# The first two tiles of an attention step change places in program order

## The chip, the core and the metric

The kernel runs on one core of a Trainium2 chip. A core has five engines with an instruction queue each: TensorE (PE, the matrix unit; its weight loads are shown as PEld), VectorE (DVE), ScalarE (ACT), GpSimd (POOL) and SyncE (SP, which issues most DMAs). Engines meet through semaphores. The metric is the time of one execution on the device in microseconds; the median of several runs is compared.

## The reference

A layer norm feeds two branches that are multiplied at the end: attention with 32 heads of 16 dimensions over 2048 tokens, and a gelu feed-forward of width 1376 with a silu on top.

```python
def _A_ref(x, wqkv, wo):           # S = 2048, D = 512, H = 32, Dh = 16
    qkv = (x @ wqkv).reshape(B, S, 3, H, Dh).transpose(2, 0, 3, 1, 4)
    q, k, v = qkv[0], qkv[1], qkv[2]
    scores = jnp.einsum("bhqd,bhkd->bhqk", q, k) * (Dh ** -0.5)
    p = _softmax(scores, axis=-1)
    o = jnp.einsum("bhqk,bhkd->bhqd", p, v)
    return o.transpose(0, 2, 1, 3).reshape(B, S, D) @ wo

xn = _layernorm(x, axis=-1)
s = _A_ref(xn, A_wqkv, A_wo)
g = _silu(_B_ref(xn, B_w1, B_b1, B_w2, B_b2))
return x + s * g
```

## The kernel before

Everything is in fp32 with operands rounded to a fast fp32 form; where accuracy asks for it a number is kept as a high and a low part, laid one below the other in the contraction (three times 16 rows make the 48 rows of a score matmul).

Attention is cut into 32 units. A unit `u` is a group of four heads (`u // 4`) and a chunk of 512 queries (`u % 4`). For each unit two things are computed from queries and keys:

- Row scores, to find the maximum of each query's scores before any exponential is taken. A tile of 128 queries by 512 keys is one matmul (`s_mm`, line 183) into a PSUM bank, and VectorE reduces it to maxima (`s_max`, line 189). When a unit has its 64 tiles, its maxima are reduced once more and negated (`nm`, line 247), split on GpSimd (lines 250 and 251), turned round by a matmul (`s_end1`, line 267), copied (`mh`, line 277) and sent through DRAM into two extra rows of the unit's queries. So the row scores of a unit have to be done before its transposed scores.
- Transposed scores, 128 keys by 512 queries, with the negated maximum added by those two rows (50 rows in all). `t_one` (line 732) does one matmul (line 739) into a PSUM bank and one exponential on ScalarE (line 741) into `slot`. Those exponentials are multiplied by the values in `pv_step` (line 798): 4 matmuls in the code, 8 on the engine (line 804), on column quarters of the array, with all 128 rows. After 16 key tiles the sum is taken out by ScalarE (`os`, line 811).

The first half of the kernel does the projections, the feed-forward and the row scores of the first nine units. The second half is one loop of 512 steps (line 966, 16 steps for each unit), and all of the change lies there. A step does four transposed tiles of a key tile (one for each head), the `pv` product of the step before, and as many row-score maxima as are due: `due(n) - due(n - 1)` is 3 in nearly all steps until the maxima are used up, and 0 in the last ones. `ORDER` spells the program order of such a step by letters:

- `T`, four times: `t_one`. The first two (T0, T1) use rows 64 to 113 of the array, the last two (T2, T3) rows 0 to 49.
- `S`, twice: a whole 512-wide row-score tile with its maximum; the first of a step (S0) is on rows 0 to 47, the second (S') on rows 64 to 111.
- `X` and `Y`: the two 256-wide halves of a third row-score tile, X on rows 0 to 47, Y on rows 64 to 111, into one bank; the maximum follows Y. Y is held until X is done.
- `V`: `pv_step` of the step before, and then, when it is due, the `s_end1` matmul of a unit.

Matmuls on different halves of the rows can run at the same time, and each brings its own weight load. The scheduling is by hand (`manual_schedule`): what the loop calls first stands first in each engine's queue. PSUM banks go round in rings. Row scores have three banks (`s_ring`), so S' of a step takes the bank of the third maximum of the step before, and S0 that of the S0 before. Transposed tiles have four (`t_tile`, line 724: one of `ps_m`, three of `ps_t`), so each takes the bank of the same tile of the step before, whose exponential must have read it.

Other work hangs on the tiles of a step by `todo`: what is put at position `i` is issued right behind tile T`i`. At position 0 there are `o_move` (DMAs on SP) and `o_den` (line 830: a reciprocal on VectorE, line 832, and two DMAs on SP), each once a unit; the loads of keys, queries and maxima are at position 3.

```python
    for n in range(L + 1):
        ua, ka = divmod(n, 16)
        want = due(n) - due(n - 1)
        i = 0
        for op in ORDER[want] if n > 1 else ("TTTTV", "TTSTSVT")[n]:
            if op in "SXY":
                s_op(op)
            ...
            else:
                if EARLY <= 4 * n + i < 4 * L:
                    t_one(ua, ka, i % 2, 1 - i // 2)
                for f, args in todo.get((n, i), []):
                    f(*args)
                i += 1
```

Of the kernel before, what the change touches and what calls it, by code (L numbers as in the profile page):

```python
# [36 lines left out]
FILL0 = 30  # L37
HB = 4
W2B = 2
ORDER = {0: "TTTTV", 3: "STXTTSTYV"}  # L40
HC = CH // 2
PAIRED = 28
KB = 3
# [5 lines left out]
def fused(ctx: ExitStack, tc: tile.TileContext, x, wqk, wv, wo, w1, b1, w2, b2, out):  # L49
# [916 lines left out]
# [6 lines that stand above are left out]
# [67 lines left out]
```

## Time and profile before

| | us |
|---|---|
| median of 3 runs | 1590.65 (1590.64 to 1590.91) |
| the profiled execution | 1590.04 |
| its span, first to last instruction | 1588.3 |

The granted TensorE clock was 1.0 throughout. A row of the page's first part gives an engine's busy time, its share of the span and its number of instructions. A row of the stretches gives, after the length, the busy time and count of each engine (or of one source line alone), then the granted clock, the busy share of the DMA engines and GB/s. A row of the timeline gives start, duration, engine, line, operation, output and inputs with shapes, how many instructions were merged into it, and in brackets idle time of the engine before it with the engine that the profile names as the releaser. Busy times of neighbours overlap, since engines are pipelined: an exponential lasts about 0.6 us and the next can start about 0.5 us after it.

### The profile page before, as it was taken

The numbers are of one execution on the slowest core, as the hardware profiler recorded it, in microseconds if no ns is written. First come the engines' busy times: TensorE is split into PE (matmuls) and PEld (weight loads), VectorE is DVE, ScalarE is ACT, GpSimd is POOL, SyncE is SP. The second block draws the span as 40 slices with busy tenths as digits, with TensorE's granted clock in tenths as the row PEclk, the third lists the DMA queues.
The fourth block names the chain that finished last, engine by engine and source line by source line (L and its number), as shares of the span: only waits on it lengthen the run. The fifth ranks groups of instructions, "written<-read, shape, count | busy, mean of one in ns | idle before, by whom it ended". The sixth has DMA issues, their size and how long they took to land.

```text
span 1588.3 us, 31761 instructions
## 1 busy us (share of the span) xinstructions
PE 1581.8 (100%) x12144; PEld 934.7 (59%) x12144; DVE 1379.1 (87%) x2261; ACT 1259.1 (79%) x2520; POOL 373.7 (24%) x394
## 2 busy tenths in 40 slices
PE   9999999999999999999999999999999999999998
PEld 8899999999894444444444444444444444444445
DVE  7599898989889999999999999999999999999734
ACT  4334343434349999999999999999999999999984
POOL 4145575756640011001000100100100000000143
PEclk9999999999999999999999999999999999999999
DMA  6626343454332123112410511411150111110252
GB/s 206 150 59 161 109 137 99 157 139 134 114 96 59 37 42 59 28 38 47 76 31 25 70 41 30 62 39 29 33 76 21 32 29 36 36 29 22 59 192 101
DMA packets 74648, 116.87 MB, mean 74 GB/s; under 512 B 23012, under 2 KB 24292, under 8 KB 73320
## 3 DMA queue, kind: packets, MB, share of 16 engines
q1 hardware_dynamic: 70748, 101.89, 23.7%
q0 software_dynamic: 3264, 12.35, 4.5%
q8 instruction: 96, 1.57, 0.4%
q10 hardware_dynamic: 484, 0.60, 0.1%
q14 instruction: 56, 0.46, 0.1%
HBM read 84.35 MB, written 25.97 MB: 69 GB/s over the span
## 4 chain that ended last, share of the span: by engine, by line
PE 97%; ACT 1%; DVE 1%; issue 0%; DMA 0%; ACTq 0%; DVEq 0%
PE pv L804 33%; PE ps L183 24%; PE ps L590 12%; PE pst L739 10%; PE pst L590 7%; PE ps L739 3%; PE ps L80 3%; PE pv L590 2%; PE ps L458 1%; ACT slot L741 1%; PE pst L80 1%; DVE st L417 0%; PE pst L440 0%; DMA xt<-in_x 0%; PE pst L458 0%
## 5 line engine op out<-in xcount | busy, mean ns | idle before, releaser
L189 DVE TENSOR_REDUCE mx<-ps 128x2 f32<-128x512 f32 x2048 | 1299.5, 684 | 144.6 <-PE pst L739 35.2
L741 ACT ACTIVATE slot<-pst 128x512 f32<-128x512 f32 x1533 | 831.7, 614 | 17.8 <-PE pst L739 9.6
L804 PE MATMUL pv<-slot,vsb 128*32 128x512 f32 x4096 | 545.4, 605 | 0.0
L183 PEld LDWEIGHTS ps<-kt,slot 48*128 48x128 f32 x1364 | 223.8, 184 | 280.2 <-DVE mx L189 278.3
L183 PE MATMUL ps<-kt,slot 48*128 48x512 f32 x1364 | 379.4, 365 | 0.0
L739 PE MATMUL pst<-qt,kt 50*128 50x512 f32 x1149 | 376.0, 436 | 0.5 <-DVE gt L672 0.3
L741 ACT ACTIVATE slot<-ps 128x512 f32<-128x512 f32 x515 | 316.5, 615 | 2.5 <-PE ps L183 0.2
L590 PE MATMUL ps<-slot,w1h 64*128 64x512 f32 x1088 | 218.1, 393 | 0.0
L739 PEld LDWEIGHTS pst<-qt,kt 50*128 50x128 f32 x1149 | 188.6, 184 | 41.8 <-ACT slot L865 12.6
L183 PE MATMUL ps<-kt,qz 48*128 48x512 f32 x512 | 212.7, 415 | 0.0
L183 PEld LDWEIGHTS ps<-slot,slot 48*128 48x128 f32 x598 | 98.3, 184 | 121.5 <-DVE mx L189 120.7
L183 PE MATMUL ps<-slot,slot 48*128 48x512 f32 x598 | 166.0, 364 | 0.0
L739 PE MATMUL ps<-qt,kt 50*128 50x512 f32 x387 | 162.7, 422 | 0.0
L590 PEld LDWEIGHTS ps<-slot,w1h 64*128 64x128 f32 x1088 | 151.5, 185 | 8.4 <-ACT junk L604 2.6
L804 PEld LDWEIGHTS pv<-slot,vsb 128*32 128x32 f32 x4096 | 80.8, 108 | 109.2 <-issue 100.2
L590 PE MATMUL ps<-slot,w1l 64*128 64x512 f32 x544 | 141.9, 393 | 0.0
L377 POOL TENSOR_TENSOR hl<-hg,hh 128x512 fp32r<-128x512 f32 x76 | 96.8, 1295 | 129.7 <-ACT hh L376 85.9
L250 POOL CAST nmh<-nm 128x16 fp32r<-128x16 f32 x32 | 6.3, 196 | 477.4 <-DVE nm L247 409.3
L739 PE MATMUL pst<-qt,slot 50*128 50x512 f32 x384 | 113.4, 421 | 0.0
L604 ACT ACTIVATE junk<-ident_r 1x1 f32<-1x1 f32 x92 | 18.0, 196 | 116.5 <-PE pst L590 113.3
L183 PEld LDWEIGHTS ps<-kt,qz 48*128 48x128 f32 x512 | 93.8, 183 | 16.3
L842 POOL TENSOR_TENSOR ot<-ot,dn 64x512 f32<-64x512 f32 x15 | 19.6, 1304 | 299.7 <-DMA dn<-den_d 256.9
(159 smaller groups left out, 1757.7 us busy)
## 6 DMA issues: line engine op xcount, KB each, us to landing
raw<-in_w SPq DMA_DIRECT2D x88, 256.0 KB
qk_h<-hh SPq DMA_DIRECT2D x32, 256.0 KB
qk_l<-hl SPq DMA_DIRECT2D x32, 256.0 KB
qt<-qk_h SPq DMA_DIRECT2D x128, 64.0 KB
slot<-qk_h SPq DMA_DIRECT2D x92, 64.0 KB
g_d<-gt POOLq DMA_DIRECT2D x16, 256.0 KB, 3.5
qt<-qk_l SPq DMA_DIRECT2D x64, 64.0 KB
dn<-den_d SPq DMA_DIRECT2D x32, 128.0 KB
```

The costliest lines, as they stand in the source:

```text
L80: nc.tensor.matmul(ps, lhs[a], rhs[b], start=first and n == 0, stop=last and n == 2)
L183: return nc.tensor.matmul(ps[:, c0:c0 + w], QS[u][r, p, qi * P:(qi + 1) * P], kts[u // NCH % KB][p][r, k0:k0 + w], start=True, stop=True).ins
L189: nc.vector.tensor_reduce(MX[u][:, 2 * p:2 * p + 2, qi, ki][:, heads, parts], ps.rearrange("p (n c) -> p n c", c=HC), axis=AX.X, op=OP.max)
L250: nc.gpsimd.tensor_copy(hl[:, 0], nm)
L377: nc.gpsimd.tensor_sub(hl, raw, hh.bitcast(F32))
L458: nc.tensor.matmul(pq["q", g, c], W1[g][i][:, k * P:(k + 1) * P], (xh, xl)[j][c][:, k], start=n == 0 and k == 0, stop=n == 2 and k == KT - 1)
L590: i = nc.tensor.matmul(ps, lhs[r], rhs[r], start=first, stop=last).ins
L604: i = nc.scalar.activation(junk[:, :1], ident_r[:1, :1].bitcast(F32), AF.Copy).ins
L739: nc.tensor.matmul(ps, kts[g % KB][p][r, k * P:(k + 1) * P], QT[u][r, p, :], start=True, stop=True)
L741: nc.scalar.activation(PT[u, k][:, 2 * p + a, :], ps, AF.Exp, scale=SCALE)
L804: nc.tensor.matmul(PV[u][32 * j:32 * j + 32, :], vsb[:, k, h:h + 32], PT[u, k][:, j, :], start=(k == 0), stop=(k == NT - 1))
L842: eng.tensor_mul(ot[c][rs, g // 2], ot[c][rs, g // 2], DN.pop(u)[rs])
```

## The change

In the order of a step with three maxima the first two letters change places: T0 is issued ahead of S0, where it was issued behind it. What hangs on T0 (position 0) is then also ahead of S0. Everything else, the number of instructions, the banks and the waits of each instruction, stays.

```diff
-ORDER = {0: "TTTTV", 3: "STXTTSTYV"}
+ORDER = {0: "TTTTV", 3: "TSXTTSTYV"}
```

## The prediction

> **What bounds the kernel now.** I read the page first, then busy time over the stage that the change touches, then a few steps in the timeline, at last windows so narrow that merged runs fall apart into single instructions.
>
> ```profile
> span 1588.3 us, 31761 instructions
> PE 1581.8 (100%) x12144; PEld 934.7 (59%) x12144; DVE 1379.1 (87%) x2261; ACT 1259.1 (79%) x2520; POOL 373.7 (24%) x394
> ```
>
> The next three rows are one stretch: all engines, then TensorE's line 804 alone, then ScalarE's line 811 alone.
>
> ```profile
> 498.00:1500.00 1002.00, 1002.00 (x7709) 451.92 (x7705) 916.93 (x1507) 992.11 (x1954) 75.07 (x124) 1.00 0.20 40
> ...
> 498.00:1500.00 1002.00, 512.05 (x3848) 75.76 (x3848) 1.00 0.20 40
> ...
> 498.00:1500.00 1002.00, 18.95 (x30) 1.00 0.20 40
> ```
>
> A step issues 8 matmuls at line 804, so the stretch holds 3848 / 8 = 481 steps, nearly all with the changed order: 2.08 us each. PE is busy 100%, ACT 99%, DVE 92%. Three engines near full mean that a share names no owner; the steps must be followed.
>
> ```profile
> 1001.06 1.07 PE L804 MATMUL pv<-slot,vsb 128*32 128x512 f32 x8
> 1002.06 0.18 PEld L183 LDWEIGHTS ps<-slot,slot 48*128 48x128 f32 x1 [0.84 <-DVE mx L189]
> ...
> 1003.08 1.07 PE L804 MATMUL pv<-slot,vsb 128*32 128x512 f32 x8
> ...
> 1004.07 0.18 PEld L183 LDWEIGHTS ps<-slot,slot 48*128 48x128 f32 x1 [0.84 <-DVE mx L189]
> ...
> 1005.16 1.07 PE L804 MATMUL pv<-slot,vsb 128*32 128x512 f32 x8
> 1006.16 0.18 PEld L183 LDWEIGHTS ps<-slot,slot 48*128 48x128 f32 x1 [0.84 <-DVE mx L189]
> ```
>
> Call the steps A (from 1002.06), B (1004.07) and C (1006.16). The label at a step's first load names DVE, but the load comes 1.00, 0.99 and 1.00 us behind the start of the pv group before it, whatever DVE does: it waits for the pv group to leave the array. What varies is the way from that load to the next pv group: 1.01 to 1.02 us in A, 1.09 in B. Fast and slow steps alternate, 2.02 and 2.08 from pv to pv, 4.10 a pair. Why is B slow?
>
> ```profile
> 1002.06 0.49 PE L183 MATMUL ps<-slot,slot 48*128 48x512 f32 x1
> 1002.06 0.50 PE L739 MATMUL pst<-qt,kt 50*128 50x512 f32 x1
> ...
> 1002.59 0.69 DVE L189 TENSOR_REDUCE mx<-ps 128x2 f32<-128x512 f32 x1 [0.20 <-PE pst L739]
> 1002.62 0.60 ACT L741 ACTIVATE slot<-pst 128x512 f32<-128x512 f32 x1
> ...
> 1003.12 0.59 ACT L741 ACTIVATE slot<-pst 128x512 f32<-128x512 f32 x1
> 1003.59 0.60 ACT L741 ACTIVATE slot<-ps 128x512 f32<-128x512 f32 x1
> 1004.07 0.62 ACT L741 ACTIVATE slot<-pst 128x512 f32<-128x512 f32 x1
> ...
> 1004.74 0.18 PEld L739 LDWEIGHTS pst<-qt,kt 50*128 50x128 f32 x1
> 1004.75 0.18 PEld L183 LDWEIGHTS ps<-slot,slot 48*128 48x128 f32 x1
> 1004.76 0.47 PE L739 MATMUL pst<-qt,kt 50*128 50x512 f32 x1
> ```
>
> A's first pair starts together on the two row halves. DVE takes up the S tile at 1002.59, ACT the T tile at 1002.62. ACT then runs A's four exps, 0.50, 0.47 and 0.48 apart; the fourth ends at 1004.07 + 0.62 = 1004.69. B's fourth T needs that bank (four T banks in turn), and its weights load at 1004.74, 0.05 later. Its matmul shows 0.47 instead of the usual 0.40: it really ran 0.07 late. The pv group at 1005.16 waits for it. So a ScalarE chain over two steps sets the pair:
>
> 0.56 (pair to first exp) + 1.45 (to the fourth) + 0.62 (it) + 0.05 + 0.42 (T load to pv) + 1.00 (pv to the next pair) = 4.10 us, from 1002.06 to 1006.16.
>
> TensorE alone needs 2 x 2.01 = 4.02. The ACT chain owns the difference.
>
> **The change, part by part.** Nothing is added or removed; in every step with three maxima T0 goes ahead of S0. They sit on different row halves (T0 on 64 to 113, S0 on 0 to 47), both behind the same pv drain. Behind them X, T1, T2, S', T3, Y keep their order, S0 still uses the same bank and T0 too, so no bank is asked for earlier than now. On PE the swap is free but for the tiny lag between two pair starts (both print 1002.06, so under 0.01): X follows S0 on its half and inherits it in fast steps. Bounds 0 to 240 x 0.01 = 2.4 us; I take 0.7.
>
> What moves is who is served first. In the program matmul completions are counted by one counter, in order: DVE waits for S0's count, ACT for T0's. Today S0 is the first count, and ACT starts 0.03 behind DVE. The next step shows the same:
>
> ```profile
> 1004.61 0.69 DVE L189 TENSOR_REDUCE mx<-ps 128x2 f32<-128x512 f32 x1
> 1004.64 0.60 ACT L741 ACTIVATE slot<-pst 128x512 f32<-128x512 f32 x1
> ```
>
> The matmuls' lengths (0.49, 0.50) explain a hundredth of it; the rest I read as the spacing of two completions. Swapped, ACT starts 0.03 earlier and DVE 0.03 later. The ACT chain becomes 4.07.
>
> The Trainium skill ("TensorE: Matmul & The Clock Gate", section "The cost: per-tile semaphore tail") says that semaphore increments of concurrent matmuls are written one after another, about 26 ns each, and that matmuls finish in program order. These rows agree with a spacing, at 0.03; by 0.026 the pair gain below would be 5.5 us instead of 6.3.
>
> DVE now pays. Its chain from A to C:
>
> ```profile
> 1003.20 0.68 DVE L189 TENSOR_REDUCE mx<-ps 128x2 f32<-128x512 f32 x1
> ...
> 1003.79 0.68 DVE L189 TENSOR_REDUCE mx<-ps 128x2 f32<-128x512 f32 x1
> ...
> 1004.53 0.18 PEld L183 LDWEIGHTS ps<-slot,slot 48*128 48x128 f32 x1
> ...
> 1004.65 0.40 PE L183 MATMUL ps<-slot,slot 48*128 48x512 f32 x1
> ...
> 1004.89 0.28 PE L183 MATMUL ps<-slot,slot 48*128 48x256 f32 x1
> ...
> 1002.87 0.28 PE L183 MATMUL ps<-slot,slot 48*128 48x256 f32 x1
> ```
>
> A's third max ends at 1004.47 and frees the bank of B's S', whose weights load at 1004.53. From there: at most 0.12 to its matmul, 0.24 to Y, 0.21 from Y to pv (1002.87 to 1003.08 in A, where nothing else is late), 1.00: C's pair could stand at 1006.10, a chain of 4.04. Plus 0.03: 4.07, level with ACT's new 4.07. The 0.12 is an upper end (T1 ahead on the same half ends about there too); by T3, whose matmul really began 0.09 behind its load, it is 4.04. So DVE has just enough room, and a regular pair falls from 4.10 to 4.07.
>
> How many pairs? Line 811 runs 30 times in the stretch, once per 16 steps: an extra ACT instruction.
>
> ```profile
> 810.54 0.63 ACT L811 ACTIVATE os<-pv 128x512 f32<-128x512 f32 x1
> ...
> 811.01 0.65 ACT L741 ACTIVATE slot<-ps 128x512 f32<-128x512 f32 x1
> ```
>
> There the exps follow `os` on ACT at 0.47, not T0's completion, so that step gains nothing. Of the 15 others 7 pairs gain: 30 x 7 x 0.03 = 6.3 us (4.2 to 8.4 with 0.02 to 0.04, as rows are rounded).
>
> The work hung on T0 (position 0: `o_move`, `o_den`) also moves ahead of S0. Its DMA issues keep their place: the SP and POOL sequences come out unchanged. The reciprocal of `o_den` moves one max forward on DVE:
>
> ```profile
> 794.22 0.69 DVE L189 TENSOR_REDUCE mx<-ps 128x2 f32<-128x512 f32 x1 [0.23 <-PE ps L739]
> 794.83 0.24 DVE L832 RECIPROCAL dr<-dr 128x16 f32<-128x16 f32 x1
> 794.99 0.63 DVE L189 TENSOR_REDUCE mx<-ps 128x2 f32<-128x512 f32 x1
> ```
>
> Today it pushes the second max from 0.61 to 0.77 behind the first, 0.16 in DVE's chain. Ahead of the first max it falls into the idle 0.23 and is hidden; without that cover it would cost 30 x 0.16 = 4.8 at most if DVE owned those pairs. What it waits for, `dr`, was sent eight steps before. Bounds: a gain of 0 to 3.0 (30 x (0.16 - 0.06, DVE's room under 4.10)); I take 0.6, since only recips in the first step of a pair matter. Against it, each unit has DVE extras (`nm`, `mh`) where DVE may already own a pair and the 0.03 is a loss: 0 to 60 x 0.03 = 1.8; I take 0.9.
>
> Sum: -6.3 + 0.7 - 0.6 + 0.9 = -5.3 us. The profiled execution took 1590.04 (span 1588.3): 1584.7. It lies 0.6 under the median 1590.65, so against the runs I forecast 1585.3.
>
> **The rivals.**
> - No change: the third chain closes the gap. If fast steps lengthen by what slow ones lose (X's lag nearer 0.01, S' at 0.12, DVE extras at their upper ends), -4.2 + 2.4 + 1.8 = 0: 1590.65. For it: three engines over 90%. Against: ACT's chain stands 0.08 a pair above TensorE's own 4.02.
> - DVE becomes the owner: slower. It decides once S' starts more than 0.15 behind its load (4.04 - 0.12 + 0.03 + 0.15 = 4.10). With the full 0.18 of a load before the matmul the DVE chain is 4.13: +0.03 x 210 = +6.3, 1597. For it: that load already follows the max by 0.06. Against: the row has 0.12, and T3's 0.09.
> - X stalls behind S0. S0 and X now stand next to each other in program order on one row half.
>
> ```profile
> 1002.17 0.19 PEld L183 LDWEIGHTS ps<-slot,slot 48*128 48x128 f32 x1
> ```
>
> X's load starts at 1002.17, inside S0's matmul, so today it is hidden. If it came only behind S0's matmul, X, T2 and T3 would be up to 0.18 later in each step: 481 x 0.18 = 87 us, 1677. Against: T0 between them is on the other half and can't be what hides it. The Trainium skill (same page, section "The mechanism") has a load overlap a running matmul only where the row groups differ; that row shows an overlap within one row half, so the measurement decides.
>
> **How the numbers follow.** A measurement of this kernel can tell 0.2%, 3.2 us, from no change. Forecast 0.70, of which 0.02 falls short of 3.2 us; no change 0.19; DVE the owner 0.09; X stalls 0.02. Faster 0.68, same 0.21, slower 0.11. Range: low end all gains at their upper bounds (-8.4 - 0.6 = -9.0): 1581.6; high end the no-change case: 1590.7. That leaves out the two slower rivals and the largest recip gain.
>
> **What would show it.** Right: in a step's first pair ACT starts ahead of DVE by 0.03; two steps from load to load take 4.07; the fourth T's load still comes 0.05 behind the exp's end; reciprocals lie before a step's first max; idle time of DVE before its maxima changes, PE stays 100%. Wrong: ACT still behind DVE (the spacing belongs to the tile, not the order); pairs still 4.10 with S' late; any fast step above 2.05; loads of X behind 0.3 us.

## The result and the profile after

| | median, us | runs |
|---|---|---|
| before | 1590.64 | 1590.40 to 1590.91 |
| after | 1583.54 | 1583.10 to 1584.09 |

The ratio is 0.9956 with a 95% interval of 0.9943 to 0.9968: 7.1 us or 0.44% faster. The profiled execution after the change took 1583.63 us. The first rows of its page:

```profile
span 1581.8 us, 31761 instructions
...
PE 1574.7 (100%) x12144; PEld 944.7 (60%) x12144; DVE 1382.3 (87%) x2261; ACT 1257.0 (79%) x2520; POOL 373.3 (24%) x394
```

The shares say nothing: TensorE is still "100%" busy. Where the time went is seen in the view of one source line, here line 804 (count, shortest, middle and longest duration in ns, then the start of its first and last instruction in us). Before:

```profile
L804 PE MATMUL pv<-slot,vsb x4096: 592/593/618, 477.5 to 1566.7; 128*32 128x512 f32 x196
```

After:

```profile
L804 PE MATMUL pv<-slot,vsb x4096: 592/593/618, 477.8 to 1560.1; 128*32 128x512 f32 x196
```

The loop took 1089.2 us from its first pv to its last, and takes 1082.3: 6.9 of the 7.1 us lie in it. Now the timeline of the kernel after, cut so narrow that single instructions show; a slow step starts at 1000.91, the next at 1002.98, the one behind it at 1004.99.

```profile
1000.68 0.68 DVE L189 TENSOR_REDUCE mx<-ps 128x2 f32<-128x512 f32 x1
1000.89 0.62 ACT L741 ACTIVATE slot<-pst 128x512 f32<-128x512 f32 x1
1000.91 0.18 PEld L739 LDWEIGHTS pst<-qt,kt 50*128 50x128 f32 x1 [0.84 <-ACT slot L741]
1000.91 0.50 PE L739 MATMUL pst<-qt,kt 50*128 50x512 f32 x1
1000.92 0.49 PE L183 MATMUL ps<-slot,slot 48*128 48x512 f32 x1
...
1001.42 0.18 PEld L183 LDWEIGHTS ps<-slot,slot 48*128 48x128 f32 x1
1001.45 0.60 ACT L741 ACTIVATE slot<-pst 128x512 f32<-128x512 f32 x1
1001.48 0.43 PE L183 MATMUL ps<-slot,slot 48*128 48x512 f32 x1
1001.49 0.69 DVE L189 TENSOR_REDUCE mx<-ps 128x2 f32<-128x512 f32 x1
1001.56 0.18 PEld L739 LDWEIGHTS pst<-qt,kt 50*128 50x128 f32 x1
...
1001.60 0.46 PE L739 MATMUL pst<-qt,kt 50*128 50x512 f32 x1
...
1002.98 0.18 PEld L739 LDWEIGHTS pst<-qt,kt 50*128 50x128 f32 x1 [0.84 <-ACT slot L741]
...
1004.99 0.18 PEld L739 LDWEIGHTS pst<-qt,kt 50*128 50x128 f32 x1 [0.84 <-ACT slot L741]
```

Three things are to be seen. ScalarE now takes up the first tile at 1001.45, 0.03 to 0.04 ahead of VectorE at 1001.49, where it was 0.03 behind. The fourth T still waits for ScalarE: the fourth exponential of the step before ends at 1000.89 + 0.62 = 1001.51, the weights load at 1001.56, the matmul shows 0.46 instead of 0.39 to 0.40. The pair from 1000.91 to 1004.99 takes 4.08, where the one shown before took 4.10. VectorE is close behind: the third maximum ends at 1001.36, S' loads at 1001.42, and its matmul too is a little stretched (0.43).

The rows shown are typical. Over some 400 steps of the loop in the two traces, the median lead is 0.034 for VectorE before and 0.035 for ScalarE after; the fourth T's load comes 0.05 behind the end of the exponential of its bank in both; and the median pair of the stretch 498 to 1500 takes 4.11 before and 4.08 after. The traces also hold the times at which the matmuls' counter was raised: before, for S0 at 1002.567 and for T0 at 1002.601; after, for T0 at 1001.426 and for S0 at 1001.461. Nowhere in either trace do two of these counts lie closer than 0.034.

A label shows how little a releaser's name can mean: the first load of a step used to sit idle 0.84 us "for DVE", now it sits idle 0.84 us "for ACT". The load comes 0.99 to 1.00 us behind the start of the pv group either way (here 1001.99 to 1002.98), so it is the same wait. The name is that of the semaphore that the first tile's load carries: VectorE's for S0, ScalarE's for T0.

### The profile page after: what moved, and what is told of

The parts are those of the page before. It is cut to its first block, busy times and chain, and to the rows that moved or that the text cites. A ratio compares the mean times of both kernels' runs of the same rounds, so it can differ in the third digit from the quotient of the medians.

```text
span 1581.8 us, 31761 instructions
## 1 busy us (share of the span) xinstructions
PE 1574.7 (100%) x12144; PEld 944.7 (60%) x12144; DVE 1382.3 (87%) x2261; ACT 1257.0 (79%) x2520; POOL 373.3 (24%) x394
## 4 chain that ended last, share of the span: by engine, by line
PE 98%; DVE 1%; DMA 0%; issue 0%; ACT 0%; DVEq 0%
PE pv L804 33%; PE pst L739 22%; PE ps L590 13%; PE ps L183 9%; PE pst L590 7%; PE ps L739 7%; PE ps L80 3%; PE pv L590 2%; PE ps L458 1%; PE pst L80 1%; DVE st L417 0%; PE pst L440 0%; DMA xt<-in_x 0%; PE pst L458 0%; DVE slot L75 0%
## 5 line engine op out<-in xcount | busy, mean ns | idle before, releaser
L739 PEld LDWEIGHTS ps<-qt,kt 50*128 50x128 f32 x387 | 71.1, 184 | 45.6 <-ACT slot L741 39.8
```

The lines of the kernel that those rows point to most:

```text
L739: nc.tensor.matmul(ps, kts[g % KB][p][r, k * P:(k + 1) * P], QT[u][r, p, :], start=True, stop=True)
```

## The experiments

Each time stands beside runs of the kernel before on the same chip, whose median lay between 1590.23 and 1590.54.

**1 and 2: the two tiles, and what hangs on T0, each alone.** In the first only the tiles change places, in the second only the hung work (`o_move`, `o_den`) moves ahead of S0.

```diff
 # tiles only (order TSXTTSTYV)
             if op in "SXY":
                 s_op(op)
+                if op == "S" and i == 1:
+                    for f, args in todo.pop((n, 0), []):
+                        f(*args)
...
-                for f, args in todo.get((n, i), []):
-                    f(*args)
+                if i or want != 3:
+                    for f, args in todo.get((n, i), []):
+                        f(*args)
```

```diff
 # hung work only (order STXTTSTYV)
             if op in "SXY":
+                if op == "S" and i == 0:
+                    for f, args in todo.pop((n, 0), []):
+                        f(*args)
                 s_op(op)
```

> T0 ahead of S0, but what hangs on T0 (o_move, o_den with its reciprocal) stays behind S0 as in the kernel before. Theory (the order of the first two completions moves ScalarE's chain forward by 0.03): nearly the whole gain stays, 1583.5 to 1585, since the reciprocal was costed at 0.6 us. Rival (the gain comes from the hung work, above all 30 reciprocals that move into DVE's idle time): back at 1589 or above.

> S0 ahead of T0 as before, but what hangs on T0 goes ahead of S0. Theory: 1590 to 1590.7, only the reciprocals' 0 to 0.6 us are gained. Rival (the hung work makes the gain): near 1584.

Measured: the tiles alone 1585.22 us (1584.97 to 1585.27; ratio 0.9967, 0.9955 to 0.998), the hung work alone 1589.99 (ratio 0.9997, 0.9988 to 1.0006). So the tiles bring 5.2 us and the hung work by itself nothing that is clear of noise, 0.5. But together they bring 7.1, not 5.7: behind the swapped tiles the hung work is worth 1.7 to 1.9 (1.7 between the two medians, whose run ranges don't meet; 1.9 when each is taken against its own runs of the kernel before). The reason is the reciprocal. With the tiles alone it still stands between a step's first and second maximum; VectorE's rows, then the first loads of the steps:

```profile
991.76 0.69 DVE L189 TENSOR_REDUCE mx<-ps 128x2 f32<-128x512 f32 x1 [0.17 <-PE ps L183]
992.37 0.24 DVE L832 RECIPROCAL dr<-dr 128x16 f32<-128x16 f32 x1
992.53 3.14 DVE L189 TENSOR_REDUCE mx<-ps 128x2 f32<-128x512 f32 x5
...
991.19 0.18 PEld L739 LDWEIGHTS pst<-qt,kt 50*128 50x128 f32 x1 [0.84 <-ACT slot L741]
993.21 0.18 PEld L739 LDWEIGHTS pst<-qt,kt 50*128 50x128 f32 x1 [0.84 <-ACT slot L741]
995.35 0.18 PEld L739 LDWEIGHTS pst<-qt,kt 50*128 50x128 f32 x1 [0.84 <-ACT slot L741]
```

That pair takes 4.16. In the kernel after, the same reciprocal lies ahead of the maxima:

```profile
991.06 0.24 DVE L832 RECIPROCAL dr<-dr 128x16 f32<-128x16 f32 x1
991.32 3.90 DVE L189 TENSOR_REDUCE mx<-ps 128x2 f32<-128x512 f32 x6
...
990.74 0.18 PEld L739 LDWEIGHTS pst<-qt,kt 50*128 50x128 f32 x1 [0.84 <-ACT slot L741]
992.76 0.18 PEld L739 LDWEIGHTS pst<-qt,kt 50*128 50x128 f32 x1 [0.84 <-ACT slot L741]
994.82 0.18 PEld L739 LDWEIGHTS pst<-qt,kt 50*128 50x128 f32 x1 [0.84 <-ACT slot L741]
```

4.08, like a pair without one. 30 reciprocals at 4.16 - 4.08 = 0.08 would be 2.4 us; 1.7 to 1.9 were measured.

The means over many units say the same. Take a step from the start of one pv group to the next and average each of the 16 steps of a unit over units 2 to 29. Seven of the 16 are the slow ones that can gain. With the tiles alone six of them get shorter, by 0.03 to 0.04 each, and the one behind the reciprocal gets longer, from 2.10 to 2.13. With the whole change that one gets shorter too, to 2.06. The seven together save 0.222 us a unit, or 7.1 for 32 units, the whole measured gain; the other nine together change by 0.002. In each of the other 15 steps the tiles alone and the whole change differ by 0.007 at most, so `o_move`, which hangs on another step than the reciprocal, plays no part.

**3 and 4: program order or row half?** T0 sits on the upper row half and S0 on the lower, so the new order could matter because of the place. Both orders were run with the halves of all tiles of the loop exchanged.

```diff
-                s_whole(whole.pop(), 1)
+                s_whole(whole.pop(), 0)
...
-                s_whole(whole[0], 0)
+                s_whole(whole[0], 1)
...
             ps, pool = s_tile(True)
-            x = s_mm(ps, cut[0], 0, 0, cut[1] * HC, HC)
+            x = s_mm(ps, cut[0], 1, HC, cut[1] * HC, HC)
...
-            s_mm(ps, job, 1, HC, n * HC, HC)
+            s_mm(ps, job, 0, 0, n * HC, HC)
...
-                    t_one(ua, ka, i % 2, 1 - i // 2)
+                    t_one(ua, ka, i % 2, i // 2)
```

> Old order, S0 first, but the two row halves are exchanged for all tiles of the loop: S0, X, T2, T3 on the upper half, T0, T1, S', Y on the lower. Theory (program order decides who is served first): as before, 1590 to 1591, and DVE starts 0.03 ahead of ScalarE in the first pair. Rival (the lower row half is always served first): T0 is now served first, so about 1584, ScalarE ahead.

> New order, T0 first, with the two row halves exchanged for all tiles of the loop: T0 is on the lower half now. Theory (program order): as after the change, 1583 to 1584.5, ScalarE 0.03 ahead of DVE. Rival (row half): also ScalarE ahead here, and the change itself, where T0 was on the upper half, would have brought nothing; a third possibility, a gain from order and half together, would give clearly less than 1583.

Measured: old order 1590.50 (ratio 1.0, 0.9991 to 1.0008), new order 1583.12 (ratio 0.9955, 0.9942 to 0.9967). The timeline of the old order with exchanged halves still has VectorE first:

```profile
1002.87 0.69 DVE L189 TENSOR_REDUCE mx<-ps 128x2 f32<-128x512 f32 x1 [0.20 <-PE pst L739]
...
1002.90 0.60 ACT L741 ACTIVATE slot<-pst 128x512 f32<-128x512 f32 x1
```

and the new order ScalarE:

```profile
1002.72 0.60 ACT L741 ACTIVATE slot<-pst 128x512 f32<-128x512 f32 x1
...
1002.75 0.69 DVE L189 TENSOR_REDUCE mx<-ps 128x2 f32<-128x512 f32 x1 [0.18 <-PE ps L183]
```

The place plays no part that these runs can tell. In all four kernels, of two matmuls that run side by side, the engine that waits for the one issued second is served 0.03 later.

**5: S0 later still.** Order `TXSTTSTYV`: X goes between T0 and S0.

> Order T X S in place of T S X: T0 first, S0 third. S0's matmul now follows X's 256 columns on its half, so its completion and VectorE's first maximum come about 0.12 later again. Theory (after the change VectorE's chain over two steps, 4.04 to 4.07, stands level with ScalarE's 4.07): VectorE owns the pairs, 0.09 to 0.12 more for each of 210, 18 to 25 us slower than the change, 1602 to 1609. Rival (VectorE still has ample room): within 3 us of the change.

Measured: 1596.00 us, 5.5 slower than before (ratio 1.0036, 1.0022 to 1.005) and 12.5 slower than the change. The direction is the theory's, the size is not. VectorE's first maximum and the steps' first loads:

```profile
1001.72 0.69 DVE L189 TENSOR_REDUCE mx<-ps 128x2 f32<-128x512 f32 x1 [0.25 <-PE ps L183]
...
1001.06 0.18 PEld L739 LDWEIGHTS pst<-qt,kt 50*128 50x128 f32 x1 [0.84 <-ACT slot L741]
1003.08 0.18 PEld L739 LDWEIGHTS pst<-qt,kt 50*128 50x128 f32 x1 [0.84 <-ACT slot L741]
1005.20 0.18 PEld L739 LDWEIGHTS pst<-qt,kt 50*128 50x128 f32 x1 [0.84 <-ACT slot L741]
```

The maximum starts 0.66 behind the first load, where it started 0.58 behind it after the change (1001.49 - 1000.91): 0.08 later, not 0.12. The pair takes 4.14, 0.06 more than after the change, and 0.06 for each of 210 pairs is 12.6 us, near the 12.5 measured. VectorE owns it now, so without the 0.08 its chain stands at 4.06: just under the change's 4.08. (With X ahead of S0 the ring also hands out the banks in another order, but S' still takes that of the third maximum, so the chain that counts here is the same.)

**6 and 7: a lighter VectorE, in both orders.** In the loop the maxima are taken over 448 of 512 columns, with the exponentials' scale at an eighth.

```diff
-        nc.vector.tensor_reduce(..., ps.rearrange("p (n c) -> p n c", c=HC), axis=AX.X, op=OP.max)
+        nc.vector.tensor_reduce(..., ps.rearrange("p (n c) -> p n c", c=HC)[:, :, :HC - 32 if "seen" not in prog else HC], axis=AX.X, op=OP.max)
...
-        nc.scalar.activation(PT[u, k][:, 2 * p + a, :], ps, AF.Exp, scale=SCALE)
+        nc.scalar.activation(PT[u, k][:, 2 * p + a, :], ps, AF.Exp, scale=SCALE / 8)
```

> Kernel before, with the maxima of the loop taken over 448 of 512 columns (224 of each half) and the exponentials' scale at an eighth, so that part of the maxima is left out; VectorE's chain is some 0.2 us a pair shorter. Theory (ScalarE's chain owns the pairs before the change): no more than 2 us faster than before, 1588.5 to 1590.7. Rival (VectorE owns them): 8 us or more faster.

> The change, with the same lighter maxima (64 of 512 columns left out, scale an eighth). Theory: ScalarE's chain at 4.07 and TensorE's own 4.02 to 4.04 a pair are left, so 0 to 3 us faster than the change, 1580.5 to 1583.5; against the old order with lighter maxima a gain of 7 to 8.5 us. Rival (VectorE alone owns the pairs after the change): 1578 or below.

Measured: old order 1589.62 (ratio 0.9995, 0.9986 to 1.0004), new order 1582.31 (ratio 0.9948, 0.9933 to 0.9963). Relief on VectorE is worth 0.9 us before the change and 1.2 after it, so VectorE does not own the regular pairs in either. With the lighter maxima in both orders the change is worth 7.3.

**8, 9, 11 and 12: a heavier VectorE, in all four combinations.** One small copy a step is added behind the first maximum. The two tiles and the hung work are then moved together (9) or one at a time (11 and 12), by the edits of 1 and 2.

```diff
                 s_whole(whole[0], 0)
+                nc.vector.tensor_copy(junk2, ident_r[:, :32].bitcast(F32))
```

> Kernel before, with one extra VectorE copy of 128x32 a step, right behind the first maximum; it only adds work. VectorE's chain grows by some 0.1 to 0.15 a pair to 4.15 to 4.2 and owns the pairs. Theory: 10 to 25 us slower than before. Rival (VectorE has ample room): under 3 us slower.

> The change, with the same extra VectorE copy a step. Theory: where VectorE owns the pairs the swap only costs, 0.03 a pair: 5 to 8 us slower than the old order with the extra copy, so the sign of the change turns round. Rival (the swap helps by itself, whoever owns the pair, as by fewer waits on TensorE): still 5 us or more faster than the old order with the copy.

> The extra VectorE copy a step, T0 ahead of S0, and what hangs on T0 behind S0 as in the kernel before: the swap of the two tiles alone under a loaded VectorE. In the run of the change with the copy a regular pair of steps took 4.14, in that of the old order with it 4.11, but the whole was 4.8 us faster. Theory (regular pairs lose 0.03 by the swap once VectorE owns them; the moved reciprocals, some 0.08 each and more, are what made the whole faster): regular pairs 4.14, pairs with a reciprocal about 4.22, 1610 to 1615, slower than the old order with the copy (1607.95). Rival (the swap alone helps here too): 1604 or below.

> The extra VectorE copy a step, S0 ahead of T0 as before, but what hangs on T0 ahead of S0. Theory: regular pairs stay at 4.11 and the pairs with a reciprocal fall from 4.18 to 4.21 to about 4.11, so 1601 to 1605.5, 2.5 to 6 us faster than the old order with the copy. Rival (the reciprocals' place is worth nothing here either, as without the copy): 1607 to 1609.

| with the copy | hung work behind S0 | hung work ahead of S0 |
|---|---|---|
| S0 first | 1607.95 (1607.56 to 1610.21) | 1598.92 (1597.51 to 1600.36) |
| T0 first | 1612.27 (1611.37 to 1613.99) | 1603.18 (1602.42 to 1603.87) |

Against the kernel before, the ratios by rows of the table are 1.0112 (1.0097 to 1.0127), 1.0055 (1.004 to 1.007), 1.0137 (1.012 to 1.0154) and 1.0079 (1.0063 to 1.0096).

The whole change (from the upper left to the lower right) was still 4.8 us faster, against the expectation. Taken apart, the expectation about the tiles holds: with a loaded VectorE the swap of the tiles costs 4.3 us in each column. It is the hung work that brings 9.0 and 9.1 in the two rows, more than the 2.5 to 6 expected of the reciprocals' place alone. The first loads of regular pairs, S0 first:

```profile
1001.24 0.18 PEld L183 LDWEIGHTS ps<-slot,slot 48*128 48x128 f32 x1 [0.84 <-DVE mx L189]
1003.25 0.18 PEld L183 LDWEIGHTS ps<-slot,slot 48*128 48x128 f32 x1 [0.84 <-DVE mx L189]
1005.35 0.18 PEld L183 LDWEIGHTS ps<-slot,slot 48*128 48x128 f32 x1 [0.84 <-DVE mx L189]
```

and with the whole change, where the copy's place on VectorE stands below:

```profile
1001.53 0.18 PEld L740 LDWEIGHTS pst<-qt,kt 50*128 50x128 f32 x1 [0.84 <-ACT slot L742]
1003.65 0.18 PEld L740 LDWEIGHTS pst<-qt,kt 50*128 50x128 f32 x1 [0.84 <-ACT slot L742]
1005.67 0.18 PEld L740 LDWEIGHTS pst<-qt,kt 50*128 50x128 f32 x1 [0.84 <-ACT slot L742]
...
1002.71 0.17 DVE L216 COPY junk<-ident_r 128x32 f32<-128x32 f32 x1
1002.79 1.28 DVE L189 TENSOR_REDUCE mx<-ps 128x2 f32<-128x512 f32 x2
```

4.11 against 4.14, which are also the commonest pairs of the two traces: 0.03 more a pair, where without the copy the swap saves. The copy puts 0.08 into VectorE's chain; without it that chain would stand at 4.06, the same figure as in the run with X between.

The old order with the copy came out inside its range (17.4 slower, 10 to 25 expected), but by luck: its regular pair takes 4.11 as without the copy, so VectorE has only drawn level there. By the same step means as in 1 and 2, the time is lost in a few steps of a unit, mainly the one behind the reciprocal (2.10 to 2.19) and the third after that one (2.04 to 2.35). Why the hung work's place matters so much there is the subject of the last section.

**10: the evacuation of pv halved between two engines.** On top of the change.

```diff
-                nc.scalar.activation(OS[u], pv, AF.Copy)
+                nc.scalar.activation(OS[u][:, :HC], pv[:, :HC], AF.Copy)
+                nc.vector.tensor_copy(OS[u][:, HC:], pv[:, HC:])
```

> The change, with the evacuation of pv at the end of a unit (line 811, 30 times) split in two halves by columns, one on ScalarE and one on VectorE, as the last unit has it. ScalarE's extra 0.47 in that step becomes about 0.25, VectorE gets some 0.35 extra in its chain. If ScalarE owns that step alone: 30 x 0.2 = 6 us faster, 1577.5. If VectorE's chain, level since the change, takes over: between 3 us faster and 3 us slower.

Measured: 1589.47 us, 5.9 slower than the change (ratio to before 0.9995, 0.9985 to 1.0004). Worse than any of the cases expected. A row of its groups by line:

```profile
L812 DVE COPY os<-pv 128x256 f32<-128x256 f32 x31 | 13.2, 425 | 13.6 <-ACT os L811 13.5
```

VectorE's half waits for ScalarE's half, 13.5 us in all or 0.45 each, and then takes 0.425. The halves run one after the other, and the wait blocks VectorE's queue with the maxima behind it. The wait stands in the program: in the trace this copy waits for ScalarE's semaphore, not for TensorE's. What put it there, and how the split would do without it, is not shown. No kernel here that takes all the maxima beat the change by more than the runs can tell.

## Why the prediction was right

Forecast were 1585.3 us, -5.3 (range 1581.6 to 1590.7); measured 1583.54, -7.1.

- *ScalarE's chain over two steps owns the pair.* Shown from two sides: relief of VectorE hardly helps before the change (0.9 us), and the fourth T's load sticks to the end of the exponential at 0.05 in both kernels. Shorter exponentials, which would show it directly, were not tried.
- *The first completion is served 0.03 earlier, by program order.* Shown by the exchanged halves and by the times of the counts. The rival that the spacing belongs to the tile, or to the row half, is out.
- *Pairs from 4.10 to 4.07.* The pair shown goes from 4.10 to 4.08, the median pair from 4.11 to 4.08. The saving, 0.03, is right; the levels were read from one pair and are a hundredth low.
- *VectorE's chain comes to 4.04 to 4.07 and has just room.* Two independent loads give 4.06. The rival "DVE the owner" describes what happens 0.02 a pair further on: then the swap costs 4.3 us.
- *X behind S0 on one half.* No stall is seen; the fast steps still take 2.01 (1002.98 to 1004.99). The 0.7 us taken for X's lag in fast steps isn't seen either: the means of the five fast steps of a unit that take 2.01 to 2.02 differ by 0.003 at most, one upwards and four downwards.
- *The sum.* It came out 1.8 us short, and its terms can be set right one by one with the step means. The gain of the pairs was sized 0.8 low: 30 x 7 x 0.03 = 6.3, where 32 units at 0.222 give 7.1. The two losses set against it, 0.7 for X's lag and 0.9 for VectorE's extras, don't show. And the hung work, "I take 0.6, since only recips in the first step of a pair matter", is no gain on top of the pairs: in the old order it is worth 0.5, not clear of noise; behind the swap it is worth 1.7 to 1.9, and that is the seventh pair, which would otherwise lose. The bounds (0 to 3.0) held it; the value taken was that of the kernel before, where VectorE still had its room. The swap uses up that room, and a reciprocal in the middle of the chain then shows in its pair. So 5.2 for the tiles alone is six pairs of a unit that gain and one that loses, and that it lies near the forecast without the hung work (6.3 - 0.7 - 0.9 = 4.7) is luck.

## What to carry to other kernels

When several engines are near full, shares name no owner; follow one bank from its release to its next use over as many steps as the pattern repeats, and compare the chains of the engines to a hundredth of a microsecond. Here two matmuls that ran side by side were counted one after the other, 0.034 us apart, in program order. So put the one whose consumer owns the step first, as long as the other consumer has more slack than the spacing. Such a gain takes the slack from the other engine, and small work that was free on it, like a reciprocal, starts to cost: look again where it stands in the queue.

## What was not expected of the hardware

The added VectorE copy of 128x32 takes 0.17 us, but it could last up to 1.2, and then a GpSimd operation ran. From the timeline of the old order with the copy:

```profile
877.25 1.27 POOL L844 TENSOR_TENSOR ot<-ot,dn 64x512 f32<-64x512 f32 x1 [31.32 <-DMA dn<-den_d]
...
877.36 1.20 DVE L216 COPY junk<-ident_r 128x32 f32<-128x32 f32 x1
```

The copy ends at 878.56, just behind GpSimd at 878.52: it was held for the whole of it. That multiplication waits for the DMA that the reciprocal starts, so the reciprocal's place in the queue shifts it against the copies. The copy's group of that kernel (busy time, mean in ns):

```profile
L216 DVE COPY junk<-ident_r 128x32 f32<-128x32 f32 x491 | 96.6, 197 | 3.2 <-DMA g_d<-gt 3.2
```

and with the hung work ahead:

```profile
L216 DVE COPY junk<-ident_r 128x32 f32<-128x32 f32 x491 | 87.6, 179 | 3.2 <-DMA g_d<-gt 3.2
```

The busy time differs by 9.0 us, as much as the two kernels. With T0 first the match is gone. The same two rows there, hung work behind and ahead of S0:

```profile
L216 DVE COPY junk<-ident_r 128x32 f32<-128x32 f32 x491 | 98.0, 200 | 3.2 <-DMA g_d<-gt 3.2
...
L216 DVE COPY junk<-ident_r 128x32 f32<-128x32 f32 x491 | 92.6, 189 | 3.2 <-DMA g_d<-gt 3.2
```

These differ by 5.4 us, the kernels by 9.1. The step means show two places where the hung work acts. With it ahead, the step behind the reciprocal is 0.10 shorter (2.19 to 2.09 with S0 first, 2.21 to 2.11 with T0 first), some 3 us over the units. The third step after that one, in which most of the held copies lie, is 0.26 and 0.19 shorter. So the reciprocal's own place and the held copies share the 9.0; how they share it is not shown, and the second part exists only with the added copy.

The Trainium skill ("Advanced Engine Details and Errata", section "GPSIMD Details") says that GpSimd and VectorE share a read and a write interface and conflict when the VectorE instruction is in a 2-port mode or has two inputs in SBUF, the memory on the chip. That one small copy here waited out a whole operation, 1.20 of 1.27 us, agrees with such a conflict; no run shows in which mode the copy ran. The maxima, which read PSUM, do not stretch: in the old order with the copy 148 of them overlap a GpSimd operation in the stretch 498 to 1500, and none took longer than 0.69 us, like the others.
